# GpSimd's weight sums beside VectorE's transposes, a key load on SyncE, and an earlier hash in a hashed-attention plus PReLU-MLP kernel

## The chip, the cores and the metric

One core of one Trainium2 chip runs the whole kernel in one launch. The metric is the device time of that core in microseconds (us); lower is better. The traces name the engines PE (TensorE; PEld is its weight load), DVE (VectorE), ACT (ScalarE), POOL (GpSimd) and SP (SyncE, which here only issues DMA transfers).

## The reference: what is computed

Attention in which a query sees only the keys of its own hash bucket, then a two-layer MLP with a PReLU between the layers:

```
q, k, v: (4, 8, 768, 64)   proj: (64, 6)
q_bits = (q @ proj > 0);  k_bits = (k @ proj > 0)          # 6 bits make a bucket
mask   = q_bucket[:, :, :, None] == k_bucket[:, :, None, :]
scores = where(mask, q @ k.T / 8, -1e9)
attn   = softmax(scores);  a = attn @ v                     # then (B,H,S,D) -> (3072, 512)
h = a @ w_in          # w_in (512, 2048)
g = max(h, 0) + alpha * min(h, 0)
out = g @ w_out       # w_out (2048, 512)
```

## The kernel before

Two heads of one batch make a **pair**; there are 16 pairs (`NPAIR`), worked one after another in the loop over `pi`. After that loop comes the MLP, written as seven-product block multiplications (class `Product`, line 901), which this change does not touch.

In one pair the work is this. `scores` (L767) makes 12 cells, each 128 keys by 384 queries by two heads: four matmuls, two of them on bf16 hash codes and two on the values. ACT turns each cell into exponentials (L770). The cells live in a ring of three double PSUM banks (`two_banks`, tag `sc`, three buffers); hashes, first transposes and the row totals use the same ring. `attend` multiplies with v (L800), `totals` makes row totals (L814) from sums of the exponentials that DVE has added up (L778 to L789). The pair's totals are divided out in the next pair's iteration by `divide`: DVE transposes of the totals (`st`, L830), an addition (`rc`, L831), two reciprocals (L833), then four small POOL copies that exchange halves (`rr`, L836 and L837), `vs` (L840), then what `between` holds (for pairs after the first: the transpose of the next k, `weight_clamp`, `weight_parts`, `add_first`), then the transpose `dn` (L842), which reads what POOL copied, and the product `x` (L848), which frees the attention's PSUM.

Beside this, each pair prepares two pieces of the weights, numbers i = 2 pi and i + 1 of a list that mixes w_in and w_out. `load_weight` (L582) brings one in as `raw`; `weight_abs` (L596 on ACT), `weight_clamp` (L606), `weight_parts` (L612) and `weight_sum` (L637, L640), all on DVE but the first, round it. When four pieces of w_in are there, `weight_group` puts four sums (L658, on POOL) and a store of the group (L663, four DMAs on SP) on the list `sums_due`; `weight_sums(count, after)` takes the next sums from it. `after` names a tile: a copy of one column of it into `late_sum` (L675) runs first on POOL, so that the sum cannot start before that tile is written. With the list's order the four groups are complete in iterations 3, 6, 9 and 12, and each group's four sums are spread over two or three iterations. In iterations 11, 12, 13 and 15 DVE also runs `sum_x` (L873).

For the hash of the next pair, `hash_bits(pi + 1)` runs PE matmuls (L729), one ACT sign (`kb`, L735) and six DMAs issued from POOL (L740, L742) that move codes across partitions.

What orders the work: `do(...)` pins an instruction behind the one that was traced before it on its engine. Plain `dma_start` calls are not pinned: the planner puts them in the queue of their engine when their inputs are ready, the earliest traced first. So the order of `do` lines in the source is the order of each compute engine, and transfers settle between them.

At the start, pair 0's q and k come in two halves on SP and ACT, pair 1's q on SP (`load(1, "q")`) and pair 1's k on POOL's queue (`load_blocks(1, "k", nc.gpsimd)`, L512); then weight piece 0, v of pair 0, pieces 1 and 2, v of pair 1 and q and k of pair 2 follow on SP. PE turns the first halves, hashes them, turns the second halves, makes three cells ahead (`ahead`), then hashes the second half (`hash_bits(0, second, DVE)`), and goes on with the other nine cells. ACT runs in its order the three exponentials, the two signs of the second hash (L748), `weight_abs(0)` (which reads piece 0), then the other nine exponentials.

## Time and profile before

| what | us |
|---|---|
| median of 3 runs | 878.25 (878.03 to 878.51) |
| the profiled execution, its own time | 881.05 |
| its span, first to last instruction | 879.3 |
| PE busy | 863.8 |
| DVE busy | 757.9 |
| ACT busy | 366.9 |
| POOL busy | 99.4 |

The profiled execution took 2.8 us more than the median of the plain runs, and 1.75 us of its own time lie outside its span. The granted TensorE clock was 0.997. The attention loop fills the first 330 us or so, the MLP the rest. PE's busy time includes overlapping matmuls, so what a change can give back is looked for in the gaps between its instructions, pair by pair, not in its share of busy time. The 16 iterations each take about 19 us, and DVE is nearly full in them (18.02 us busy in the 19 us from 30 to 49).

### The profile page before, as it was taken

The numbers are of one execution on the slowest core, as the hardware profiler recorded it, in microseconds if no ns is written. First come the engines' busy times: TensorE is split into PE (matmuls) and PEld (weight loads), VectorE is DVE, ScalarE is ACT, GpSimd is POOL, SyncE is SP. The second block draws the span as 40 slices with busy tenths as digits, with TensorE's granted clock in tenths as the row PEclk, the third lists the DMA queues.
The fourth block names the chain that finished last, engine by engine and source line by source line (L and its number), as shares of the span: only waits on it lengthen the run. The fifth ranks groups of instructions, "written<-read, shape, count | busy, mean of one in ns | idle before, by whom it ended". The sixth has DMA issues, their size and how long they took to land.

```text
span 879.3 us, 15198 instructions
## 1 busy us (share of the span) xinstructions
PE 863.8 (98%) x5706; PEld 576.9 (66%) x5706; DVE 757.9 (86%) x1215; ACT 366.9 (42%) x654; POOL 99.4 (11%) x215
## 2 busy tenths in 40 slices
PE   8999999999998999999999999999999999999996
PEld 4444444444444445559996558996557997557996
DVE  5999999999998978899897769898668989668986
ACT  6877878878666752221112222112222112222111
POOL 2221322224223301120000000000000000000000
PEclk9999999999999999999999999999999999999999
DMA  9766797798896617585433425334434333520242
GB/s 207 178 148 135 178 237 163 150 249 194 210 266 146 208 60 264 202 312 216 141 127 90 170 87 200 111 117 122 141 121 155 139 120 89 185 85 1 96 152 69
DMA packets 167875, 137.23 MB, mean 156 GB/s; under 512 B 122944, under 2 KB 151312, under 8 KB 164208
## 3 DMA queue, kind: packets, MB, share of 16 engines
q1 hardware_dynamic: 160000, 123.25, 49.6%
q0 software_dynamic: 5376, 11.74, 4.1%
q10 hardware_dynamic: 2416, 1.18, 0.6%
q8 instruction: 47, 0.77, 0.4%
q14 instruction: 36, 0.29, 0.1%
HBM read 104.87 MB, written 28.31 MB: 151 GB/s over the span
## 4 chain that ended last, share of the span: by engine, by line
PE 67%; DVE 11%; issue 3%; ACT 2%; DMA 2%; SPq 0%; DVEq 0%; ACTq 0%
PE sc L767 4%; PE av L800 4%; PE f_0a L901 2%; PE z_4a L901 2%; PE z_7a L901 2%; PE z_3a L901 2%; PE z_6a L901 2%; PE z_5a L901 2%; PE f_4a L901 2%; PE f_2a L901 2%; PE f_1a L901 2%; PE f_3a L901 2%; PE z_2a L901 2%; PE f_5a L901 2%; PE z_1a L901 2%
## 5 line engine op out<-in xcount | busy, mean ns | idle before, releaser
L767 PE MATMUL sc<-qT,kT 64*128 64x384 f32 x768 | 156.7, 487 | 0.0
L770 ACT ACTIVATE pt<-sc 128x768 f32<-128x768 f32 x192 | 153.1, 811 | 6.0 <-PE sc L767 5.2
L800 PE MATMUL av<-pt,vn 128*32 128x385 f32 (+1 forms) x1536 | 127.4, 486 | 0.0
L800 PEld LDWEIGHTS av<-pt,vn 128*32 128x32 f32 x1536 | 48.7, 109 | 77.5 <-issue 68.1
L767 PEld LDWEIGHTS sc<-qT,kT 64*128 64x128 f32 x768 | 69.1, 189 | 37.3 <-issue 36.6
L954 DVE TENSOR_TENSOR g<-g,g 128x384 f32<-128x384 f32 x128 | 68.3, 554 | 2.2
L767 PE MATMUL sc<-qb,kb 64*128 64x384 bf16 x384 | 64.1, 326 | 6.0 <-ACT pt L770 2.7
L1018 DVE TENSOR_TENSOR gs<-g,gs 128x768 f32<-128x768 f32 x56 | 53.3, 951 | 1.0
L1010 DVE TENSOR_TENSOR ws<-wl 128x512 f32<-128x512 f32 x56 | 38.4, 686 | 18.1 <-DMA wl<-w_out_s 16.2
L1018 DVE TENSOR_TENSOR gs<-g 128x768 f32<-128x768 f32 x56 | 53.2, 950 | 0.0
L596 ACT ACTIVATE wr<-raw 128x512 int32<-128x512 uint32 x32 | 22.1, 691 | 60.9 <-issue 34.1
L740 POOL DMA_DIRECT2D qb<-kb x60 | 30.0, 504 | 133.8 <-ACT kb L735 133.8
L767 PEld LDWEIGHTS <-kb 64*128 64x128 bf16 x384 | 20.2, 94 | 37.5 <-issue 9.1
L950 DVE SCALAR_TENSOR_TENSOR g<-h,alpha 128x384 f32<-128x384 f32 x32 | 19.7, 616 | 25.2 <-ACT h L943 25.1
L778 DVE TENSOR_TENSOR accp<-pt,pt 128x1536 f32<-128x1536 f32 x16 | 28.1, 1754 | 7.6 <-ACT pt L770 7.6
L783 DVE TENSOR_TENSOR accd<-accd,pt 128x1536 f32<-128x1536 f32 x16 | 28.1, 1758 | 1.7
L789 DVE TENSOR_TENSOR accd<-accd,accp 128x1536 f32<-128x1536 f32 x16 | 28.1, 1758 | 0.6
L786 DVE TENSOR_TENSOR accp<-accp,pt 128x1536 f32<-128x1536 f32 x16 | 28.0, 1753 | 0.0
L782 DVE TENSOR_TENSOR accd<-pt,pt 128x1536 f32<-128x1536 f32 x16 | 28.0, 1751 | 0.0
L901 PE MATMUL f_0a<-x,wi 128*128 128x384 f32 x64 | 23.5, 489 | 0.0
L901 PE MATMUL f_1a<-x,wi 128*128 128x384 f32 x64 | 23.3, 486 | 0.0
L901 PE MATMUL f_2a<-x,wi 128*128 128x384 f32 x64 | 23.3, 486 | 0.0
(354 smaller groups left out, 1755.2 us busy)
## 6 DMA issues: line engine op xcount, KB each, us to landing
wi<-w_in_s SPq DMA_DIRECT2D x32, 896.0 KB, 4.7
wl<-w_out_s SPq DMA_DIRECT2D x16, 1024.0 KB, 4.8
wl<-w_out_r SPq DMA_DIRECT2D x12, 1024.0 KB, 4.9
raw<-in_moe_w_out_dram SPq DMA_DIRECT2D x16, 512.0 KB, 5.0
raw<-in_moe_w_in_dram SPq DMA_DIRECT2D x16, 512.0 KB, 4.8
w_in_s<-wsi SPq DMA_DIRECT2D x16, 448.0 KB, 6.4
qn<-in_q_dram SPq DMA_DIRECT2D x64, 96.0 KB, 5.4
vn<-in_v_dram SPq DMA_DIRECT2D x16, 384.0 KB, 5.3
```

Of the source, the lines that this page charges most:

```text
L740: nc.gpsimd.dma_start(bits["q", pi][D * s : D * s + 32, cols], raw[c + 32 : c + 64, 2 * half])
L767: do(PE.matmul(sc[:, s, :CW], what["k", pi][r, ks], what["q", pi][r, qs], start=first, stop=not first,))
L770: do(ACT.activation(pts[kc][:, g, :, :CW], sc[:, :, :CW], AF.Exp, scale=SCALE / DOWN))
L778: do(DVE.tensor_tensor(accp[pi], p(0), p(1), op=ALU.add))
L782: do(DVE.tensor_tensor(accd[pi], p(3), p(4), op=ALU.add))
L783: do(DVE.tensor_tensor(accd[pi], accd[pi], p(5), op=ALU.add))
L789: do(DVE.tensor_tensor(accd[pi], accd[pi], accp[pi], op=ALU.add))
L800: do(PE.matmul(av[pi][D * s + t : D * s + t + 32, g, :w], nat["v", pi][:, s, kc * D + t : kc * D + t + 32], pts[kc][:, g, s, :w], start=(k ...
L901: do(PE.matmul(self.ps[bank], self.left(left, k), self.right(right, k), start=start and k == 0, stop=k == self.nk - 1, skip_group_check=no ...
L954: do(DVE.tensor_tensor(new_g(b, to)[:, i], g_m[b, x][:, i], g_m[b, y][:, i], op=ALU.subtract))
L1010: do(DVE.tensor_tensor(t, w2[b, n, x], w2[b, n, y], op=op))
L1018: do(DVE.tensor_tensor(t, g2[b, n, x], g2[b, n, y], op=ALU.subtract))
```

## The change

Three things:

1. **When POOL's sums run.** In `divide`, `vs` moves ahead of the four `rr` copies, and the sum is taken there, tied to `vs`; the copies now follow the sum on POOL. In the iteration's second half, the sum is tied to the result of `weight_sum(i + 1)` in place of the transposed q of pair `pi + 2`, and is taken ahead of `weight_group(i + 1)` and of the next pair's hash. A group that is completed by piece i + 1 therefore gets its first sum one place later than before.
2. **Where pair 1's k is loaded.** On SP, behind pair 1's q and ahead of weight piece 0, in place of POOL's queue.
3. **When pair 0's second hash runs.** After the first of the three cells made ahead, not after the third.

```diff
-    def load_blocks(pi, name, queue=nc.sync):
+    def load_blocks(pi, name):
...
-                queue.dma_start(
+                nc.sync.dma_start(
...
         do(DVE.tensor_tensor(dst.bitcast(I32), x, r, op=ALU.add))
+        return (dst if i < HW else dst[:, 0])[:, :1]
...
-            do(POOL.tensor_copy(late_sum, after[:, :1]))
+            do(POOL.tensor_copy(late_sum, after))
...
             do(DVE.reciprocal(rr[:, :, h], r))
+        vsum[pi] = pool.tile([P, 1], F32, name=f"vs{pi}", tag="vs")
+        do(DVE.tensor_scalar(vsum[pi], av[pi][:, 0, CW : CW + 1], EPS, None, op0=ALU.mult))
+        weight_sums(1, vsum[pi])
         for q0 in (0, D):
             q1 = q0 + 32
             do(POOL.tensor_copy(rr[q0 : q0 + 32, :, 1], rr[q1 : q1 + 32, :, 1]))
             do(POOL.tensor_copy(rr[q1 : q1 + 32, :, 0], rr[q0 : q0 + 32, :, 0]))
-        weight_sums(1)
-        vsum[pi] = pool.tile([P, 1], F32, name=f"vs{pi}", tag="vs")
-        do(DVE.tensor_scalar(vsum[pi], av[pi][:, 0, CW : CW + 1], EPS, None, op0=ALU.mult))
         between()
...
-    load_blocks(1, "k", nc.gpsimd)
+    load(1, "k")
...
-    scores(0, ahead)
+    scores(0, ahead[:1])
     hash_bits(0, second, DVE)
+    scores(0, ahead[1:])
...
-        weight_sum(i + 1)
+        weight_sums(1, weight_sum(i + 1))
         weight_group(i + 1)
...
         if pi + 2 < NPAIR:
             turn_blocks(pi + 2, "q")
-            weight_sums(1, tr["q", pi + 2])
-        else:
-            weight_sums(1)
         attend(pi)
```

## The prediction

> **What bounds the kernel now.** I read the page's busy times first, then PE's waits, then the timelines of PE, DVE and POOL pair by pair, then the issues on SP.

> ```profile
> PE 863.8 (98%) x5706; PEld 576.9 (66%) x5706; DVE 757.9 (86%) x1215; ACT 366.9 (42%) x654; POOL 99.4 (11%) x215
> ...
> PE sc L767 <- ACT pt L770: 2.7, 1, 2.7
> PE sc L767 <- DVE st L830: 2.2, 4, 1.3
> PE sc L767 <- ACT qb L748: 1.0, 2, 0.7
> ```

> PE is busy nearly throughout, so only its gaps can be won. In the list of PE's waits (engine, line, for whom: total us, times, longest) the score matmuls wait 2.2 us for DVE's transposes of the totals, because these hold a bank of the ring. From one pair's first attend matmul to the next, PE's timeline gives 19.14 to 19.15 us in the undisturbed pairs 3, 4, 7, 10 and 14. Over that: pair 2 0.17, pair 5 0.13, pair 6 0.57, pair 8 0.12, pair 9 0.59, pair 11 0.18, pair 12 1.44, pair 13 4.97; in all **8.2 us**. Pairs 6 and 9 stand behind two iterations that each had two POOL sums. Pair 5 beside pair 6, where no sum runs:

> ```profile
> 108.70 1.26 POOL L658 TENSOR_TENSOR wsi<-wsi 128x512 f32<-128x512 f32 x1
> 111.44 1.27 POOL L658 TENSOR_TENSOR wsi<-wsi 128x512 f32<-128x512 f32 x1
> ...
> 109.05 0.94 DVE L831 TENSOR_SCALAR rc<-st 128x12 f32<-128x12 f32 x1
> 110.27 0.97 DVE L703 STREAM_TRANSPOSE kT<-kn 128x768 f32<-128x768 f32 x1
> 111.16 0.64 DVE L606 TENSOR_SCALAR_CACHE_REDUCE wx<-wx 128x512 f32<-128x512 f32 x1
> 111.85 1.14 DVE L612 TENSOR_SCALAR wx<-wx 128x512 uint32<-128x512 uint32 x1
> ...
> 128.76 0.17 DVE L831 TENSOR_SCALAR rc<-st 128x12 f32<-128x12 f32 x1
> 130.79 0.43 DVE L612 TENSOR_SCALAR wx<-wx 128x512 uint32<-128x512 uint32 x1
> ...
> 128.78 0.34 PE L767 MATMUL sc<-qb,kb 64*128 64x384 bf16 x2 [0.39 <-DVE st L830]
> ```

> Columns are start, duration, engine, line. Beside a sum, L831 takes 0.94 for 0.17 and L612 1.14 for 0.43: they end where the sum ends. L606, beside the second sum's start, is not longer (0.64; 0.65 in pair 6).

> Pair 13 is another matter, and so is the start:

> ```profile
> 267.21 0.67 ACT L596 ACTIVATE wr<-raw 128x512 int32<-128x512 uint32 x1 [7.57 <-DMA raw<-in_moe_w_out_dram]
> ...
> 5.19 3.23 SPq L512 DMA_DIRECT2D qn<-in_q_dram  x4
> 8.46 1.29 SPq L582 DMA_DIRECT2D raw<-in_moe_w_out_dram  x1
> ...
> 13.85 0.68 ACT L596 ACTIVATE wr<-raw 128x512 int32<-128x512 uint32 x1
> ```

> ACT waited 7.6 us for a weight piece (issued on SP at 259.49), behind which all exponentials of pair 13 were queued. At the start ACT reaches piece 0 at 13.85, just after it landed (issued 8.46, landed 13.51).

> [...] L831 and L612 wait, L606 and transposes don't; and once POOL was the one to wait, its one-column copy taking 0.75 us for 0.18 at 264.14 beside L873, which has two inputs. [...] The share of DMA engines here is 1.04 or more in each 2 us from 4 to 20 us[...].

> **The change part by part.**

> *Sums.* Behind `weight_sum` POOL needs about 0.1 to start, 0.18 for the copy and 1.27 for the sum, so 1.6 us; DVE meanwhile runs the transpose of q (0.97) and two of st (0.60)[...], and reaches L831 after 1.53. Behind `vs` it runs kT (0.97) and L606 with its accumulator read (0.7), and reaches L612 after 1.5. So DVE gets back L831's 0.75 and L612's 0.7: over eight sums of each kind 5.8 and 5.3 by the rows, 11.1 us of DVE time. What it pays: the four rr copies (0.23 apart, 0.93 in all) now start 1.5 us later, at about 1.6 after `vs`[...]. I take 0.7. So DVE gains 0.7 in each iteration with both sums, not 1.45. That is still enough: pair 6's stall of 0.57 was 0.13 an iteration earlier, so two such iterations had built it up; halving the excess of 1.45 leaves less than the 0.3 to 0.6 that DVE idles ahead of L778 in quiet pairs. Gain on PE: pairs 5, 6, 8, 9, 11, **-1.6 us**.

> Pair 12's 1.44 is DVE late by its sums plus `sum_x` (0.92) ahead of st. The first goes, but the sum tied to `weight_sum` in iteration 11 now overlaps L873, which must wait about 0.7. I take **-0.4** (0 to -1.4). The same collision in iteration 13, and a sum in iteration 14 with no q transpose to cover it, cost **+0.4** (0 to +1.5).

> *The store of group 2.* Its four DMAs stood on SP from 236.65 to 245.11 and now become ready only after the fourth sum, near 245, behind iteration 11's q, v and k loads, ahead of the late piece that was issued at 259.49. The eight loads before it go out earlier, the stores perhaps at 250 to 255, the piece at 255 to 258; with the 5 to 7.6 us that such pieces take to land it lands at 261 to 265, and ACT wants it near 263. Pair 13's excess of 4.97 falls by **1.8**; from both sides: -4, if it lands in time; +3, if the transfers that were done at 237 to 243 now stand ahead of it on full DMA engines.

> *k on SP.* Four issues at 0.66 to 0.9 (q's four took 3.23, a later k 3.92) put piece 0's issue from 8.46 to about 11.9, and its landing, at 4 to 5 us, to near 15.9 (13.6 if the DMA engines alone decide, since what has to move ahead of it is the same; 17.4 at worst). POOL loses four issues of 0.98, which nothing waited for. k itself lands before piece 0, near 15, about when DVE turned it before (14.98). Pieces 1 and 2, both v and pair 2's q and k also issue 3 us later; attend's v landed at 14.55 and is wanted at 22, so it is covered.

> *The hash.* PE ran it from 11.70 to 12.56 and then waited 0.7 and 0.3 for the signs. One cell earlier it starts near 10.0, ACT signs between exponentials, and PE goes on with cells: about 1.1 us won on PE. But with three banks PE can be only three cells ahead of ACT, and ACT's nine exponentials stand behind `weight_abs(0)`: landing plus 0.7, then 0.81 each. The fourth of the nine cells starts at landing + 1.5; before it started at 16.25. So the gain is kept if piece 0 lands by 13.6, nothing is won at 14.75, and at 15.9 the start loses **+1.1** (-1.1 to +2.6).

> *Hash transfers of later pairs.* The six POOL DMAs (1.52 for three, 0.5 each after) are traced after the new copy that waits for `weight_sum`, but are not pinned. ACT's sign is done 7 us before `weight_sum` (iteration 4's transfers issue at 100.20, L640 ends at 107.6), so the planner should issue them first, as it put the k load's first issue at 1.36 between the two instructions that make `ident`. Cost nothing, if so.

> Sum: -1.6 - 0.4 + 0.4 - 1.8 + 1.1 = **-2.3**. On the profiled execution's own 881.05 that is 878.75 (its span 877.0); it lies 2.8 above the median, so for the median 878.25 - 2.3 = **876.0**.

> **Rivals.** *POOL's queue decides (slower).* If the last hash transfers stand behind the copy that waits for `weight_sum`, they issue at 109.2 in iteration 4 and land 1.7 to 4 us later; the second cell needs the last q codes at 108.15, so PE stalls 3 us or more in eight pairs, +24, near 900; if only the last k codes are late (wanted by the seventh cell at 112.2), 0 to 1 each, up to +8. Against it is the early readiness; it decides once a hash issue follows a sum on POOL. Chance 0.08. *The piece transfers decide (slower).* Piece 0 at its late end (+2.6) and pair 13 worse by 1 to 3, against -1.6: 880 to 882.5. For it: DMA shares near or over 1 at 4 to 20 and at 240 to 255 us. Chance 0.20. *The parts cancel (no change).* Sums bring 1.6, the start takes it, pair 13 stays: 877 to 879.5[...]. Chance 0.25. *The forecast*: 0.47, with its own range 871.5 to 876.4.

> **How the numbers follow.** A measurement of this kernel can tell about 0.2%, 1.76 us, from no change. The best ends together (start -1.1, pairs -1.6, pair 12 -1.4, pair 13 -4) would give 870; I begin the range at 871.8. The slow piece case ends it at 882.0, which leaves out the queue case and some of each edge. Faster 0.47, same 0.25, slower 0.28.

> **What would show it.** L831 near 0.2 and L612 near 0.45 in all iterations; a wait of `dn` for `rr` in eight iterations; no wait of sc for st in pairs 6 and 9; the order of L740, L742 and L675 on POOL; piece 0's landing against 14.75 and pair 0's first attend matmul against 22.04; ACT's wait for a piece in pair 13. I am wrong if the pairs still take over 19.2 us with L831 and L612 short, since then DVE was not what held them.

## The result, and the profile after

The changed kernel is 0.6% slower: 883.08 us median of 5 runs (881.93 to 886.27), against 878.51 (878.03 to 878.62) for the kernel before, measured beside it; ratio 1.0057, 95% interval 1.0036 to 1.0078. The prediction said 876.0; the result lies above the end of its range, too. Four single runs of 1008 to 2356 us (one each of e2, e7, e9 and before) are left out of the ratios and the spreads below.

In the kernel after, most lines from 641 on stand one higher than before (L767 is L768, L770 is L771, L831 is L832), the `rr` copies are L840 and L841, `vs` is L836, `dn` L843 and `sum_x` L874; in e7, e8 and e12 most of these stand one higher again. Below, a pair's **period** is the time from the previous pair's first attend matmul to its own, as in the prediction.

The profiled execution took 882.06 (span 880.2). First the busy line of its page, then two lines from its list of PE's waits (the result that waited, whom it waited for: total us, times, longest):

```profile
PE 863.0 (98%) x5706; PEld 576.0 (65%) x5706; DVE 749.2 (85%) x1215; ACT 368.0 (42%) x654; POOL 96.8 (11%) x220
...
PE sc L768 <- ACT pt L771: 7.0, 2, 4.3
PE sc L768 <- DVE st L831: 1.0, 2, 0.8
```

DVE is 8.7 us less busy than before, and PE waits less for its transposes (1.0 for 2.2). But PE's wait for exponentials rose from 2.7 to 7.0, in two pieces: 2.68 at the start, 4.28 in pair 13. Both times ACT stood before a weight piece (ACT's timeline: start, duration, line, and in brackets the idle time before and what ended it):

```profile
15.23 0.67 ACT L596 ACTIVATE wr<-raw 128x512 int32<-128x512 uint32 x1 [2.68 <-DMA raw<-in_moe_w_out_dram]
...
267.15 0.66 ACT L596 ACTIVATE wr<-raw 128x512 int32<-128x512 uint32 x1 [9.10 <-DMA raw<-in_moe_w_out_dram]
```

The profiled execution of before that the prediction used was not typical: the kernel before ran in a second trace (e10 below) with a span of 876.7 instead of 879.3. Pair 13 is 4.13 shorter there; pair 14 (0.74), the start (0.30) and the MLP take part of that back. Against that second trace the change does this, in us on PE: start +0.07, pairs 1 to 11 -1.55, pair 12 -0.41, **pair 13 +6.54**, pair 14 -0.74, the rest -0.47; sum +3.4, as the spans say (880.2 and 876.7).

### The profile page after: what moved, and what is told of

Read it like the earlier page. It is cut to its first block, busy times and chain, and to the rows that moved or that the text cites. A ratio compares the mean times of both kernels' runs of the same rounds, so it can differ in the third digit from the quotient of the medians.

```text
span 880.2 us, 15210 instructions
## 1 busy us (share of the span) xinstructions
PE 863.0 (98%) x5706; PEld 576.0 (65%) x5706; DVE 749.2 (85%) x1215; ACT 368.0 (42%) x654; POOL 96.8 (11%) x220
## 4 chain that ended last, share of the span: by engine, by line
PE 92%; DVE 3%; DMA 2%; issue 1%; ACT 1%; SPq 1%; ACTq 0%; DVEq 0%
PE sc L768 15%; PE av L801 13%; PE f_0a L902 2%; PE z_4a L902 2%; PE z_7a L902 2%; PE z_3a L902 2%; PE z_6a L902 2%; PE z_5a L902 2%; PE z_1a L902 2%; PE z_2a L902 2%; PE f_4a L902 2%; PE f_7a L902 2%; PE f_6a L902 2%; PE f_5a L902 2%; PE f_3a L902 2%; PE f_2a L902 2%
## 5 line engine op out<-in xcount | busy, mean ns | idle before, releaser
L771 ACT ACTIVATE pt<-sc 128x768 f32<-128x768 f32 x192 | 154.0, 812 | 8.3 <-PE sc L768 6.8
L768 PE MATMUL sc<-qT,kT 64*128 64x384 f32 x768 | 157.3, 488 | 0.0
L768 PEld LDWEIGHTS sc<-qT,kT 64*128 64x128 f32 x768 | 69.3, 190 | 38.4 <-issue 38.1
L768 PE MATMUL sc<-qb,kb 64*128 64x384 bf16 x384 | 63.8, 328 | 8.0 <-ACT pt L771 7.0
L596 ACT ACTIVATE wr<-raw 128x512 int32<-128x512 uint32 x32 | 22.1, 692 | 59.1 <-issue 30.2
L768 PEld LDWEIGHTS <-kb 64*128 64x128 bf16 x384 | 19.6, 95 | 38.7 <-issue 14.1
L779 DVE TENSOR_TENSOR accp<-pt,pt 128x1536 f32<-128x1536 f32 x16 | 28.2, 1760 | 17.9 <-ACT pt L771 17.9
```

Source lines behind the costliest of these rows:

```text
L768: do(PE.matmul(sc[:, s, :CW], what["k", pi][r, ks], what["q", pi][r, qs], start=first, stop=not first,))
L771: do(ACT.activation(pts[kc][:, g, :, :CW], sc[:, :, :CW], AF.Exp, scale=SCALE / DOWN))
L779: do(DVE.tensor_tensor(accp[pi], p(0), p(1), op=ALU.add))
```

## The experiments

Two theories stood against each other. **Store**: the group's store, made ready one place later, now stands on SP between the loads and the weight piece of pair 13 and keeps the piece late. **Start**: k on SP makes the loss, by what it delays behind it, and pair 13 varies by chance. Each row is one kernel; the last three columns are pair 0's first attend matmul and the periods of pairs 12 and 13, from the one trace of each.

| kernel | us | ratio to before, 95% | pair 0 | pair 12 | pair 13 |
|---|---|---|---|---|---|
| before, first trace | 878.51 | | 22.04 | 20.57 | 24.11 |
| before, second trace (e10) | 878.59 | 0.9999 (0.999 to 1.0008) | 22.34 | 20.57 | 19.98 |
| after | 883.08 | 1.0057 (1.0036 to 1.0078) | 22.41 | 20.16 | 26.52 |
| after, second trace (e11) | 882.3 | 1.0044 (1.0029 to 1.0059) | 22.13 | 20.17 | 25.80 |
| e1 sums alone | 881.28 | 1.003 (1.002 to 1.0041) | 22.37 | 20.14 | 25.33 |
| e5 k on SP alone | 879.13 | 1.0011 (1.0002 to 1.002) | 22.50 | 20.58 | 19.93 |
| e6 hash alone | 877.39 | 0.9989 (0.9983 to 0.9996) | 21.12 | 20.52 | 19.50 |
| e2 after, group first | 878.3 | 0.9992 (0.9985 to 0.9999) | 24.27 | 19.49 | 21.77 |
| e3 after, k on POOL | 880.3 | 1.0023 (1.0013 to 1.0033) | 21.00 | 20.14 | 25.33 |
| e4 = e2 and e3 | 876.02 | 0.9969 (0.9958 to 0.998) | 21.25 | 19.50 | 21.17 |
| e7 after, piece on POOL | 878.39 | 0.9992 (0.9985 to 0.9999) | 24.14 | 20.16 | 19.50 |
| e8 = e4 and e7 | 875.87 | 0.9967 (0.9955 to 0.9979) | 21.50 | 19.50 | 20.15 |
| e9 = e4, store late | 880.36 | 1.0017 (1.001 to 1.0025) | 21.03 | 19.64 | 27.30 |
| e12 = e8, sum_x later | 874.4 | 0.9954 (0.994 to 0.9968) | 21.16 | 19.15 | 19.50 |

**e1, the sums alone.** Part 1 of the change put on the kernel before; k stays on POOL's queue and the second hash at its old place.

> The first part alone: the sums' new places, with pair 1's k on POOL and the second hash as before. Theory STORE (the sums' new order lets the store of group 2 go out late, ahead of the weight piece of pair 13, ACT then waits for that piece longer, PE stands still and its clock drops): no loss at the start, the iterations up to pair 11 gain 1.6 us, pair 13 loses 2 to 6 us, so 879.5 to 884, slower or the same as before, and not below 878. Theory START (the k load on SP makes the loss, by what it delays behind it on SP): 876 to 877, faster.

Measured: 881.28. Pairs 3 to 11 take 19.15 each, and pair 13 takes 25.33. So this part alone brings both the gain in the middle and the loss in pair 13.

**e2, the group first.** In the kernel after, the group is put on the list ahead of the sum again, so that its sums and its store come as early as before:

```diff
-        weight_sums(1, weight_sum(i + 1))
-        weight_group(i + 1)
+        summed = weight_sum(i + 1)
+        weight_group(i + 1)
+        weight_sums(1, summed)
```

> The changed kernel, but weight_group(i + 1) goes ahead of the sum, so that a group completed by piece i + 1 gets its first sum in the same iteration, as before, and group 2's store is on the list in iteration 11. Theory STORE: pair 13 is as before (excess 4 to 5 us over 19.15, not 7.4), store of group 2 issued before 246; 876.5 to 878. Theory START: still 881 to 885, with pair 13 as in the changed kernel or the loss elsewhere.

Measured: 878.3, some 5 less than after and just over the expected range. The store issues at 235.51 to 243.60, and pair 13 takes 21.77, shorter than was expected. Pair 12 got 0.67 faster as well (19.49). The start was worse in this trace (24.27), which is taken up under the clock below.

**e3 and e4, k on POOL's queue**, once in the kernel after and once with e2's edit:

```diff
-    load(1, "k")
+    load_blocks(1, "k", nc.gpsimd)
```

> The changed kernel, but pair 1's k is loaded on POOL's queue as before. Weight piece 0 should land near 13.5 and pair 0's first attend matmul start near 21.0 in place of 22.41, -1.4 us at the start by both theories. Theory STORE: pair 13 keeps its loss, 880.5 to 882.5, slower than before. Theory START: 876 to 878.

> Both of these: the sums beside the transposes in the iterations they had before, the earlier hash, k on POOL. Theory STORE: start -1.0, sums -1.6, pairs 12 and 13 as before: 875 to 876.5, faster than before and than the changed kernel. Theory START: the same 875 to 877; this run is for the size of the gain, not to tell the two apart.

Measured: 880.3 and 876.02. Pair 0 stands at 21.00 and 21.25, so the hash's gain is kept once k is off SP; pair 13 falls by the group's order (25.33 in e3, 21.17 in e4). e4 beats both kernels.

**e5 and e6, k alone and the hash alone**, each on the kernel before.

> The second part alone: pair 1's k on SP, all else as before. Theory STORE, refined (piece 0 is late by the four issues ahead of it, PE stands still for over 2 us and sometimes gets a lower clock after that): piece 0 lands near 15.3, pair 0's first attend matmul starts at 23 to 25 in place of 22.04; later pairs as before, so 879.5 to 881.5. Rival (the k load also upsets SP in all later pairs, or costs nothing because only the order of the same transfers changes): over 882, or 878 to 878.8.

> The third part alone: the second hash after one cell. With piece 0 landing near 13.5 the first attend matmul starts at 20.9 to 21.3 in place of 22.04: 877.3 to 877.8, the same within the bound or just faster. Rival (ACT's nine exponentials behind piece 0 eat it): no change, 878.4.

Measured: e5 878.5 to 883.5, median 879.13, with pair 0 at 22.50: less than was expected, since k's four issues took 2.77 us and piece 0 landed at 15.17. e6 877.39 with pair 0 at 21.12, as expected. Alone, the two cancel (+1.0 and -1.0 us by the ratios). Together they don't: after is 2 to 3 us above e3, which differs from it in k alone (1.0057 and 1.0044 for 1.0023). At the start, the hash's gain is what piece 0's landing takes away: with k on POOL the earlier hash brings pair 0 from 22.37 (e1) to 21.00 (e3), with k on SP from 22.50 (e5) only to 22.41 (after).

**e7 and e8, the piece by another queue.** The store keeps its late place, and the one weight piece of pair 13 is loaded on POOL's queue; then the same in e4:

```diff
+            queue = nc.gpsimd if i == 27 else nc.sync
...
-            nc.sync.dma_start(raw[i], piece(i))
+            queue.dma_start(raw[i], piece(i))
```

> The changed kernel, but weight piece 27, for which ACT waits in pair 13, is loaded on POOL's queue and not behind the store on SP; the store stays as late as in the changed kernel. Theory STORE: ACT's wait of 9.1 us for the piece goes, PE's stall in pair 13 and the lower clock after it go with it, pair 13 takes 19.5 to 21 us in place of 26.5: 875 to 878. Rival (the late store itself loads the DMA engines, so that anything is late then): pair 13 stays over 24, 881 to 884.

> The kernel with no lag and with k on POOL, and with piece 27 on POOL's queue too. Theory STORE: pair 13 falls from 21.2 to about 19.5: 873.5 to 875. Rival (the excess left in pair 13 there is DVE's, behind sum_x): 875.5 to 876.5, as without it.

Measured in e7: the store still issues at 255.42 to 260.72, but the piece was issued on POOL at 253.74 and landed at 258.14, and pair 13 takes 19.50 for 26.52. What held the piece was therefore its place in SP's queue; the store as such, still late, does not make the loss. How much the store's transfers lengthen a landing is not shown by this run, since here the piece was issued 1.7 us ahead of the store. The median, 878.39, is a little over what was expected, because of a bad start (24.14). e8 gives 875.87, hardly less than e4 and short of its expectation: with the piece in time, pairs 13 and 14 still take 20.15 and 20.56, as the rival there said, for DVE (see e12).

**e9, the store alone made late.** e4, with the store of this one group held back one place on the list and pinned there (`skip` is an empty entry, which only takes a place); the sums stay early:

```diff
+        if n == 2:
+            sums_due.append((skip, ()))
         sums_due.append((store, ()))
...
-                nc.sync.dma_start(w_in_s[4 * c + ii][:, :, kk], w[:, :, ii])
+                pinned(n == 2, nc.sync.dma_start(w_in_s[4 * c + ii][:, :, kk], w[:, :, ii]))
```

> The kernel with no lag and with k on POOL (876.0), but the store of group 2 alone is pinned on SP to the place that it has in the changed kernel, behind the k loads of iteration 11; all sums stay where they were. Theory STORE: the place of these four transfers is enough: pair 13 goes from 21.2 to 24 to 27, 879.5 to 882.5. Rival (the loss needs the other sums' places too, or the k load on SP): 875.5 to 877.

Measured: 880.36, 4.3 more than e4 (on another chip, each against its own runs of before: 1.0017 and 0.9969), pair 13 27.30, a little over what was expected. The store's place alone is enough for the loss.

**e10 and e11, before and after once more**, unchanged, for a second trace of each.

> The kernel before once more, for its trace. The profiled execution of before took 881.05 where its plain runs take 878.4. Theory STORE holds that this execution had a rare long wait for piece 27: here pair 13 should take 19.5 to 21.5 in place of 24.11, all other pairs as before to 0.1, and the time 878 to 879. If pair 13 takes 24 again, the excess of pair 13 is before's own and the difference of the medians must lie elsewhere.

> The changed kernel once more, for a second trace. Theory STORE: pair 13 takes 24 to 28, with ACT waiting 7 to 10 us for piece 27, in this trace as well; the first attend matmul starts at 22.4 to 24.3, according to whether PE's clock falls after its stall near 15. 881 to 885. Rival (pair 13 is chance in both kernels): pair 13 at 19.5 to 21 here.

Measured: 878.59 with pair 13 at 19.98, and 882.3 with pair 13 at 25.80. After's loss repeats; before's late pair 13 doesn't, nor does it show in e5 and e6 (19.93 and 19.50), where the sums are as before. Of before's 29 plain runs in this round three took 880 or more.

**e12, sum_x later.** e8, with `sum_x` of iterations 11 to 13 moved behind the next `divide`, so that it is no longer ahead of `st`:

```diff
-        if 11 <= pi < 14 or pi == 15:
-            sum_x(0, min(pi - 11, 3), DVE)
+        if pi == 15:
+            sum_x(0, 3, DVE)
...
+        if 12 <= pi < 15:
+            sum_x(0, pi - 12, DVE)
         weight_sum(i)
```

> No lag, k on POOL, piece 27 on POOL's queue, and sum_x of iterations 11 to 13 moved behind the next iteration's divide, so that it neither delays the totals' transposes nor meets a POOL sum there. If the excess left in pairs 12 to 14 (0.35, 1.0 and 1.4 in the trace of the kernel without this) is DVE's delay through sum_x, the score matmuls' wait for st goes and it is 873 to 874; if DVE is then late with its sums of exponentials, the wait moves to the row totals and it stays at 875.5 to 876.5.

Measured: 874.4, 0.9954 of before (0.994 to 0.9968), the fastest here and just above what was expected. DVE's timeline at the end of iteration 13, e8's first:

```profile
281.32 1.56 DVE L875 TENSOR_TENSOR x<-x,x 128x768 f32<-128x768 f32 x1
282.80 0.63 DVE L832 STREAM_TRANSPOSE st<-sm 128x192 f32<-128x192 f32 x2
```

and the same transposes in e12, which come straight after q's:

```profile
279.94 0.97 DVE L705 STREAM_TRANSPOSE qT<-qn 128x768 f32<-128x768 f32 x1
280.83 0.60 DVE L832 STREAM_TRANSPOSE st<-sm 128x192 f32<-128x192 f32 x2
```

In e8 `sum_x` stood ahead of `st` and, beside a POOL sum, took 1.56 (0.95 at its new place in e12, at 288.26); in e12 nothing is between.

## Why the prediction was wrong, step by step

**The sums: right, to a tenth.** DVE and POOL in iteration 4 of the kernel after, the iteration that the prediction showed before (start, duration, engine, line; DVE's timeline, then POOL's):

```profile
107.23 0.97 DVE L704 STREAM_TRANSPOSE qT<-qn 128x768 f32<-128x768 f32 x1
108.13 0.60 DVE L831 STREAM_TRANSPOSE st<-sm 128x192 f32<-128x192 f32 x2
108.77 0.17 DVE L832 TENSOR_SCALAR rc<-st 128x12 f32<-128x12 f32 x1
...
110.80 0.43 DVE L612 TENSOR_SCALAR wx<-wx 128x512 uint32<-128x512 uint32 x1
112.06 1.76 DVE L779 TENSOR_TENSOR accp<-pt,pt 128x1536 f32<-128x1536 f32 x1 [0.83 <-ACT pt L771]
```

```profile
107.60 1.27 POOL L659 TENSOR_TENSOR wsi<-wsi 128x512 f32<-128x512 f32 x1
...
109.57 1.28 POOL L659 TENSOR_TENSOR wsi<-wsi 128x512 f32<-128x512 f32 x1
110.91 0.36 POOL L840 COPY rr<-rr 32x12 f32<-32x12 f32 x1
```

The first sum runs beside the transposes and ends at 108.87, within 0.1 us of L832's start; the second ends at 110.85, within 0.1 of L612's. L832 takes 0.17 for 0.94 and L612 0.43 for 1.14, the forecast sizes. The transposes beside the first sum take 0.97 and 0.60, as in before where no sum ran (at 127.23 and 128.12). Why L832 and L612 are longer beside a sum and the transposes are not, no run here shows. Pairs 5, 6, 8, 9 and 11 fell to 19.15, together -1.6. DVE's busy time fell by 8.7 in all, where the prediction counted 11.1. What it made DVE pay for the gain (0.7 per iteration, `dn` waiting for `rr`; an estimate that no trace had shown) did not occur here: one copy took 0.36 for 0.19, and all four were done by 111.97, before L779, which waits for ACT (0.83). No `rr` copy of this trace takes over 0.40. In e8, where this addition waits only 0.30 for ACT, one does meet it: it takes 1.80 from 286.25, and `dn` waits 0.32 for it. So the term was too large for this kernel, but it changed nothing, since DVE's extra slack has no taker: over the kernel its wait for `pt` at L779 rose from 7.6 to 17.9 us, and pair 13's stall is only a part of that.

**Pair 12 and the collision: right.** Pair 12 gained 0.42. `sum_x` in iteration 11 meets the sum, as foreseen (DVE's timeline: beside the POOL sum, which started at 241.65 and took 1.28, and in iteration 12 without one):

```profile
242.18 1.56 DVE L874 TENSOR_TENSOR x<-x,x 128x768 f32<-128x768 f32 x1
...
262.32 0.92 DVE L874 TENSOR_TENSOR x<-x,x 128x768 f32<-128x768 f32 x1
```

The +0.4 for iterations 13 and 14 is not tested by this kernel: pair 14 takes 19.14 in it, but behind the stall of pair 13.

**Hash transfers of later pairs: right.** In iteration 4 the six POOL issues end at 103.69, and the copy that waits for the sum follows at 107.45. With the pairs at 19.15, the rival of POOL's queue had no case.

**The start: right in mechanism, too large in size.** Pair 0 is +0.37 against the first trace of before and +0.07 against the second, for the forecast +1.1. Piece 0 landed at 15.21, between the break-even 14.75 and the forecast 15.9. The issues were shorter than priced (2.77 for four).

**The store of group 2: the step that failed**, -1.8 forecast, +2.4 against the profiled execution of before and +6.5 against a typical one. Three things in it were wrong.

*First, there was little to win.* Pair 13's excess of 4.97 belonged to one execution. In the second trace of before it is 0.83: the piece was issued 0.4 us earlier and landed 2.2 us sooner (7.6 and 5.8 from issue to landing), and PE waited 0.3 for the exponentials. The sum of the prediction was made against an execution 2.8 us above the median, and the most unusual pair in it was taken for the kernel's habit.

*Second, the store took the loads' place in the queue.* SP issues one DMA after the other in this stretch, about 0.1 us apart. Here are its issues (start, duration) in the second trace of before:

```profile
253.21 5.06 SPq L512 DMA_DIRECT2D kn<-in_k_dram  x4
258.37 0.62 SPq L849 DMA_DIRECT2D x_s<-x  x1
259.09 0.38 SPq L582 DMA_DIRECT2D raw<-in_moe_w_out_dram  x1
```

in the kernel after:

```profile
247.39 6.25 SPq L512 DMA_DIRECT2D kn<-in_k_dram  x4
253.74 4.23 SPq L664 DMA_DIRECT2D w_in_s<-wsi  x4
258.07 1.80 SPq L850 DMA_DIRECT2D x_s<-x  x1
259.96 2.85 SPq L582 DMA_DIRECT2D raw<-in_moe_w_out_dram  x2
```

and in e4, where the store was done by 239.59:

```profile
249.32 5.74 SPq L512 DMA_DIRECT2D kn<-in_k_dram  x4
255.16 0.59 SPq L850 DMA_DIRECT2D x_s<-x  x1
255.86 0.38 SPq L582 DMA_DIRECT2D raw<-in_moe_w_out_dram  x1
```

The k loads began 5.8 us and ended 4.6 us earlier in after, as forecast. But the store's four issues and a slower `x_s` filled that time and 0.9 us more, and the piece issued at 259.96, not at "255 to 258". So everything else came 1.9 us earlier (pair 13's period begins at 253.34 for 255.23) while the piece landed 2.1 later (267.05 for 264.93): the stall of 4.3 us in place of 0.3 is the sum of the two. The gain of 1.9 ended in front of a landing that had not moved forward with it. Of the 2.1, 0.9 is the later issue and 1.2 the longer time from issue to landing (7.1 for 5.8). In e4 the early store lets the piece move forward with the pairs.

ACT's wait for this piece, in the second trace of before, in e4, in e9 and in e7:

```profile
265.03 0.68 ACT L596 ACTIVATE wr<-raw 128x512 int32<-128x512 uint32 x1 [5.09 <-DMA raw<-in_moe_w_out_dram]
```

```profile
262.53 0.67 ACT L596 ACTIVATE wr<-raw 128x512 int32<-128x512 uint32 x1 [6.32 <-DMA raw<-in_moe_w_out_dram]
```

```profile
266.55 0.66 ACT L596 ACTIVATE wr<-raw 128x512 int32<-128x512 uint32 x1 [9.99 <-DMA raw<-in_moe_w_out_dram]
```

```profile
263.33 0.69 ACT L597 ACTIVATE wr<-raw 128x512 int32<-128x512 uint32 x1 [3.56 <-issue]
```

Some 5 us of it are harmless, as the second trace of before shows; what is beyond that reaches PE. In e7 the piece had landed 5 us before ACT took it.

*Third, a stall was priced at its own length.* PE's timeline of the kernel after at the end of the stall:

```profile
264.02 0.81 PE L768 MATMUL sc<-qT,kT 64*128 64x384 f32 x4
269.11 0.51 PE L768 MATMUL sc<-qb,kb 64*128 64x384 bf16 x2 [4.28 <-ACT pt L771]
269.38 1.51 PE L768 MATMUL sc<-qT,kT 64*128 64x384 f32 x4
```

The four matmuls that took 0.81 take 1.51 after it. The windows of that trace tell why (length, then the busy time of PE, PEld, DVE, ACT and POOL; the third column from the end is the granted clock):

```profile
262.00:266.00 4.00, 2.65 (x18) 1.17 (x17) 3.70 (x10) 0.00 (x0) 1.45 (x2) 1.00 0.97 279
266.00:270.00 4.00, 0.89 (x4) 0.63 (x5) 0.57 (x3) 2.85 (x5) 0.96 (x4) 0.69 1.05 347
270.00:274.00 4.00, 4.00 (x18) 2.04 (x16) 2.17 (x2) 2.08 (x3) 0.00 (x0) 0.50 0.88 94
274.00:278.00 4.00, 4.00 (x32) 2.47 (x30) 3.93 (x7) 3.63 (x5) 0.00 (x0) 0.96 0.95 204
```

Half of 270 to 274 is lost, 2.0 us, and some 0.6 more on both sides together. So pair 13's +6.5 is 4.0 of stall and some 2.5 of clock. The time at half clock, twice the clock's shortfall times the length of each row, comes to 2.5 + 4.0 + 0.3 = 6.8 us here; in e1 and e3, where pair 13 takes 25.33, it is 3.4. The prediction's own lines could have told it: PE waited 2.7 in pair 13 of before, and the pair's excess was 4.97 (the granted clock was 0.62 there from 270 to 274).

The rival "the piece transfers decide" (0.20) named the right mechanism for pair 13, at +1 to +3, without the clock. At the start it had piece 0 at its late end, +2.6, where the traces show +0.1 to +0.4; that its time came near the measured one is in part luck.

**What stays open.** Why the same piece takes 5.8, 7.1 or 7.6 us to land is not settled. Whether the late store's transfers lengthen it was not shown. Each kernel has one or two traces, and pair 14 moves by 0.7 to 1.4 between them. Of the 2 to 3 us between after and e3, the traces of after put 1.1 to 1.4 at pair 0 and 0.5 to 1.2 in pair 13, where its half clock lasted twice as long as e3's. How the plain runs divide it, no run isolates.

## What to carry to other kernels

When an edit makes a store ready later, find the slots that it leaves and the slots that it takes in its issuing queue: loads move up, but whatever stands behind the store's new place does not (here k's loads began 5.8 us earlier, and the piece was issued 0.9 us later). Look for the transfer that has the least slack there, and ask what happens when everything else comes earlier and it does not. Price a PE stall of a few us at its length plus the low clock that can follow (here 1.7 us in e1 and some 2.5 in after), and look at a second execution before counting on a loss that one pair shows in one trace.

## What was not expected of the hardware

After a stall near 2 us the clock came down in two traces and stayed in two others. The kernel after's start, the same in four traces, had PE waiting 2.68, 1.56, 2.13 and 2.11 us for piece 0 in after, e11, e2 and e7. The clock stayed at 1.00 in the first two and fell in the other two, where pair 0 came 1.7 to 2.1 us later. e7's windows at the start:

```profile
14.00:16.00 2.00, 0.58 (x4) 0.09 (x1) 0.93 (x3) 0.74 (x2) 0.00 (x0) 1.00 1.08 375
16.00:18.00 2.00, 1.31 (x6) 0.81 (x7) 1.47 (x4) 2.00 (x3) 0.00 (x0) 0.69 0.99 371
18.00:20.00 2.00, 2.00 (x10) 1.06 (x8) 1.97 (x3) 0.86 (x2) 0.00 (x0) 0.50 1.23 286
```

| trace | interval, us | PE busy in it | clock in it | clock in the next |
|---|---|---|---|---|
| after | 11.51 to 14.93 | 2.46 | 1.00 | 1.00 |
| after | 14.93 to 18.34 | 1.69 | 1.00 | 1.00 |
| e11 | 13.87 to 17.28 | 1.85 | 1.00 | 1.00 |
| e2 | 14.74 to 18.15 | 1.33 | 1.00 | 0.50 |
| e7 | 13.33 to 16.75 | 1.31 | 1.00 | 0.50 |
| after | 264.10 to 267.51 | 0.73 | 1.00 | 0.50 |
| after | 267.51 to 270.93 | 1.82 | 0.50 | 0.50 |
| after | 270.93 to 274.34 | 3.41 | 0.50 | 1.00 |

After's stall of 2.68 lies on both sides of 14.93, with PE busy for 2.46 and 1.69 in the two intervals; those of e2 and e7 lie almost whole in one (1.33 and 1.31). In the traces of before and after, from the start of their clock records on, the clock fell after every interval at full clock with at most 1.41 us of PE busy time, and after none with 1.69 or more. PE was not idle throughout before the fall in e2 and e7: it was busy for 1.3 of the 3.4 us. No run here moves the phase on purpose. It fits that plain runs of e7 spread from 876.25 to 879.96 and those of e2, with the same start, from 876.40 to 879.77, where the six of e8, whose start has no such stall, stay within 875.75 to 876.29.
